# One Trainium2 core, attention into routed experts: zero rows written first, a third key buffer, a ranking matmul moved

## The chip, the cores and the metric

The kernel runs on one core of one Trainium2 chip, in one launch. The metric is the device time of an execution in microseconds; of several executions the median is taken. The profile is one execution, taken by the hardware profiler. Its times are counted from the start of the span.

## What is computed

Three layers follow one another. Batch B is 2, there are 8 heads, 768 positions and 64 elements to a head, so that a token is a row of 512.

```
# attention: only the first n_global = 8 keys and the last n_local = 96 are kept
scores = q @ k.T / 8 - slope[h] * dist          # -1e9 where a key is not kept
a      = exp(scores - max);  a /= sum(a) + 1e-9
x      = a @ v                                   # rows of 512
# mixture of 8 experts, one expert to a token
logits = x @ w_gate;  gate = sigmoid(x @ w_local)
e      = argmax(logits) where gate < 0.5 (or at the first token), else that of the token before
x      = softmax(logits)[e] * (relu(x @ w1[e]) @ w2[e])
# a channel mix of neighbouring tokens
k      = relu((mu_k x + (1-mu_k) x_prev) @ w_k)
out    = sigmoid((mu_r x + (1-mu_r) x_prev) @ w_r) * (k*k @ w_v)
```

## The kernel before, in words

The tokens are cut into 12 tiles of 128 (6 to a batch). A tile of attention has four pairs of heads; the loop at line 956 goes over the 48 pairs, `i` from 0, with `t` the tile and `h` = 0, 2, 4, 6 the first head of the pair. All instructions are put in order by hand: the block is under `manual_schedule`, so every engine runs its instructions in the order in which this code emits them, and the stages of one pair are emitted in different passes of the loop. In pass `i` come, among others:

- `emit_exp(i)`: ScalarE's exponentials. `emit_min` for pairs i+1 and i+2 (odd passes): VectorE adds the bias table to the scores and keeps the minimum. `emit_pe(i-2)`: the transposed weights are copied from PSUM, by ScalarE for every third pair, else by VectorE (L769, L771).
- `emit_qT` for a later tile (L972) and `emit_kT(t+1)` where h is 0 (L977): TensorE transposes a tile of queries or keys (L672), ScalarE copies it to `qz` (L682) or `strip` (L677). Beside them stand the loads of later tiles on SyncE's queue (L655).
- `rpop()`: one step of the routing chain (below), its part called `mid`.
- `emit_pT(i-1)`: TensorE transposes the exponentials (L757, L759) into one of two PSUM banks. On even passes then `emit_qk` for pairs i+2 and i+3, the scores (L726), into two banks that the minima must have read, and `emit_pv` for pairs i-4 and i-3, the values (L783).
- the part of the routing step called `post`, if it has one, and after it loads, GpSimd's copies of the eight global keys into `strip` (`emit_kglob`, L701, L702) and the scatter of finished rows.

The routing chain is a list of steps (L824 to L864), one taken in each pass once its tiles are done: gate matmuls (`route_lg`, L181), argmax, a scan over tokens, counts, positions. After tile 5 the experts are ranked by their count so far: `order_a` (L268) builds a key and a diagonal on VectorE, `order_b` (L277) spreads the keys with a matmul (L280) and compares, ranks and makes a one-hot on VectorE (L283 to L286); `early_start` (L801) picks the first expert by a matmul (L292), copies its number (L294), and SyncE reads it to load that expert's weights (L549) while attention still runs. `order_b` is also called a second time, by `ranks`, after all tokens.

At the head (L866 to L897), before the loop: SyncE loads the first tile's keys and queries in halves, GpSimd makes index patterns (`iotas`), VectorE and GpSimd make the bias tables (`tables0`: heads 4 to 7 on GpSimd, L515, L516), and the loads of L891 follow. `vps` are two tiles that hold, for the windows, the global keys' values and the 96 rows before a tile; their first 32 rows, and the first 24 columns of the four `peb`, are set to zero by GpSimd (L893 to L896), and `load_vp` (L658) writes into `vps` behind that. In passes 1, 5, 9 and 13 ScalarE's queue writes zeros to `xs` in DRAM, two transfers of 256 KB (L1012). Keys of a tile (128 by 512, 256 KB, in rows of 256 bytes) land in one of the `kn` buffers.

Behind the loop the first expert's tiles (`fill`), which use two of the `kn` and `qn` buffers as scratch, then all experts, then the channel mix. These have no part in the change.

Of the kernel before, what the change touches and what calls it, by code (L numbers as in the profile page):

```python
# [8 lines left out]
F32 = mybir.dt.float32  # L9
# [7 lines left out]
P = 128  # L17
B, H, S, HD = 2, 8, 768, 64
D, E, F = 512, 8, 1024
NT = S // P  # L20
NTT = B * NT
# [4 lines left out]
NG = 8  # L26
CP = WIN + NG
W = CP + P
PAD = P - CP
# [503 lines left out]
def build(ctx, tc, ins, out):  # L533
    n = Net(ctx, tc, ins, out)
    nc = tc.nc
    q, k, v = ins["q"], ins["k"], ins["v"]
# [3 lines left out]
    rp = ctx.enter_context(tc.tile_pool(name="rp", bufs=1))  # L540
# [101 lines left out]
    ap = astack.enter_context(tc.tile_pool(name="ap", bufs=1))  # L642
    X, xTs, kn, qn, vn, vhl = {}, {}, {}, {}, {}, {}

    def load(nm, t, half=None):
        b, j = divmod(t, NT)
        reg = {"k": kn, "q": qn, "v": vn}[nm]
        if half is not None:
            if half == 0:
                reg[t] = ap.tile([P, H, HD], F32, tag=f"{nm}n", bufs=2, name=f"{nm}n{t}")  # L650
            hs_ = slice(half * 4, half * 4 + 4)
            nc.sync.dma_start(out=reg[t][:, hs_, :], in_=ins[nm][b, hs_, j * P:(j + 1) * P, :].rearrange("h p d -> p h d"))
            return
        d = ap.tile([P, H, HD], F32, tag=f"{nm}n", bufs=3 if nm == "v" else 2, name=f"{nm}n{t}")
        nc.sync.dma_start(out=d, in_=ins[nm][b, :, j * P:(j + 1) * P, :].rearrange("h p d -> p h d"))  # L655
        reg[t] = d

# [168 lines left out]
    for gi, g in enumerate(groups):  # L826
        def lg(t, g=g):
            n.route_lg(g, t, xTs[t], "PT" if t == NTT - 1 else "R")
            if t == g[-1]:
                n.route_max(ap2, g)  # L830

        def fin(g=g):
            n.route_pos(ap2, g)
            scq.extend(g)
            if g[-1] == FREE - 1:
                n.cnt4 = n.early_count(rp, "cnt4")
            if g[-1] == 9:
                n.cnt9 = n.early_count(rp, "cnt9")
            if g[-1] == 7:
                n.cnte = n.early_count(rp, "cnte")  # L840

        def step(pre=None, mid=None, post=None, t=g[-1]):
            rsteps.append((t, pre, mid, post))

        max2, rows, scan, cnt = (lambda f=f, g=g: f(ap2, g) for f in (n.route_max2, n.route_rows, n.route_scan, n.route_cnt))
        if gi == 0:
            step(mid=lambda lg=lg, g=g: (lg(g[0]), lg(g[1])))
        else:
            step(mid=lambda lg=lg, g=g: lg(g[0]), t=g[0])
            step(mid=lambda lg=lg, g=g: lg(g[1]))  # L850
        if gi == 5:
            step(mid=max2, post=rows)
        else:
            step(mid=max2)
            step(mid=rows)
        step(scan)
        step(mid=cnt)
        step(post=fin)
        if g[-1] == 9:
            step(mid=early_row)  # L860
        if g[-1] == NT - 1:
            step(mid=lambda: n.order_a(rp, "f", n.clast, None))
            step(mid=lambda: n.order_b(rp, "f"))
            step(mid=early_start)  # L864

    with tc.manual_schedule():  # L866
# [5 lines left out]
        peb = [ap.tile([P, 2 * P], F32, name=f"peb{i}") for i in range(4)]  # L872
# [3 lines left out]
        vps = [ap.tile([P, D], F32, name=f"vp{i}") for i in range(2)]  # L876
# [6 lines left out]
        tstack = ExitStack()  # L883
        tp = tstack.enter_context(tc.tile_pool(name="tp", bufs=1))
        n.iotas(tp)
        n.scalars(n.const)
        tq = n.tables0(ap, tp) + n.tables(ap, tp)
        first = first_half(0)
        for _ in range(6):
            tq.pop(0)()  # L890
        for nm, a in ("k1", "q1", "v0", "v1"):  # L891
            load(nm, int(a))
        for t in vps:  # L893
            nc.gpsimd.memset(t[0:PAD + NG, :], 0.0)
        for t in peb:
            nc.gpsimd.memset(t[:, 0:PAD], 0.0)  # L896
        load_vp(1)  # L897
        NP_ = len(pairs)
        early = None
# [13 lines left out]

        def fill():
            for a in range(2):
                hn = [ap.tile([P, H, HD], F32, tag=f"{nm}n", bufs=2, name=f"hn{nm}{a}").rearrange("p h d -> p (h d)") for nm in "kq"]
                eh = [ap.tile([P, H, P], F32R, tag=tg, bufs=1, name=f"e{tg}{a}") for tg in ("tb0", "tb")]
                for u in xs_tile(0, *xe[a], hn, eh, BASES[0] + a * P):
                    if u == KF + 5:
                        early_split(1) if a == 0 else first_split()  # L920
                    for _ in range(WNEXT[u]):
                        w_next()
                    yield
# [32 lines left out]
        for i in range(NP_ + 3):  # L956
            t, h = pairs[i] if i < NP_ else (NTT + (i - NP_) // 4, 2 * ((i - NP_) % 4))
            j = t % NT
            emit_pe(i - 2, "ACT")
            if i < NP_:  # L960
                emit_exp(i, pairs[i])
            emit_xT()
            if 0 <= i - 1 < NP_:
                if pairs[i - 1][1] == H - 2:
                    n.route_ri(pairs[i - 1][0], stat[pairs[i - 1][0]][1])
            for u in (i + 1, i + 2) if i % 2 else (1,) if i == 0 else ():
                if u < NP_:
                    emit_min(u, pairs[u])
            emit_pe(i - 2, "DVE")
            rpre()  # L970
            u = {1: 1, 3: NTT, 5: 2}.get(i, t + 2 if h == 6 else NTT)
            if u < NTT:  # L972
                emit_qT(u)
                if u + 2 < NTT:
                    load("q", u + 2)
            if h == 0 and t + 1 < NTT:
                emit_kT(t + 1)  # L977
                if t + 2 < NTT:
                    load("k", t + 2)
                if t == 0:  # L980
                    load("q", 2)
            if (h == 2 or i >= NP_) and xq and xq[0] <= done_x:
                n.route_x(ap, xTs[xq[0]], X, xq[0])
                xq.pop(0)
            sct = list(scq)
            post = rpop()
            if i < 5:
                warm(NDUM[2 + i], 64)
            if 0 <= i - 1 < NP_:
                emit_pT(i - 1, pairs[i - 1])  # L990
            if i % 2 == 0:
                for u in (i + 3, i + 2):
                    if u < NP_:
                        emit_qk(pairs[u])
                for u in (i - 4, i - 3):
                    if 0 <= u < NP_:
                        emit_pv(u, pairs[u])
                        if pairs[u][1] == H - 2:
                            done_x = pairs[u][0]
            if post:  # L1000
                post()
            if i == 2:
                n.routing_consts()
            if h == 6 and t + 2 < NTT:
                load("v", t + 2)
            if h == 4 and 0 < t < NTT - 1 and (t + 1) % NT:
                load_vp(t + 1)
            if i < NP_ and j < NT - 1:
                emit_kglob(t, h // 2)
            if h == 2 and t < E // 2:  # L1010
                for e in (2 * t, 2 * t + 1):
                    nc.scalar.dma_start(out=n.xs[e * REG:e * REG + PRE, :], in_=n.warm)  # L1012
            if sct and i >= next_sc:
                next_sc = i + 1
                scatter(scq.pop(0))
            if tq:
                for _ in range(NTAB[i]):
                    if tq:
                        tq.pop(0)()
                if not tq:  # L1020
                    tstack.close()
            if i == 5:
                n.gate_rest()
            if i == 6:
                n.mix_load()
            if i == 8:
                n.mix_rest()
                n.limits(n.const)
            if i == NP_:
                early_split(0)  # L1030
            if 0 in wsrc and early is None:
                early = True
                ld_q = list(range(4))
                hi_q = [None] * 2 + [(c, s) for c in range(NIN) for s in range(2)]
            if ld_q:
                w_load(0, ld_q.pop(0))
            for u in lo_q[:1]:
                w_lo1(0, *lo_q.pop(0))
                if u[1] and u[0] < 4:
                    w_load(0, 4 + u[0])  # L1040
            if hi_q:
                u = hi_q.pop(0)
                if u:
                    w_hi1(0, *u, dve=u[1])
                    lo_q.append(u)
            if i == NP_:
                fl = fill()
            if i > NP_:
                F_(DRAINF[i - NP_])
# [192 lines left out]
    k2, sig = {}, {}  # L1242
# [129 lines left out]
    with tc.manual_schedule():  # L1372
# [48 lines left out]
        hn = ztile([P, 2, D], F32, "hn")  # L1421
# [267 lines left out]
```

## Time and profile before

| | us |
|---|---|
| median of 3 runs | 534.46 (533.41 to 535.18) |
| the profiled execution | 534.88 |
| span of the profiled execution | 533.1 |
| TensorE busy | 508.9 (95%) |
| VectorE busy | 353.3 (66%) |
| ScalarE busy | 262.1 (49%) |
| GpSimd busy | 124.9 (23%) |

PE is TensorE, PEld its weight loads, DVE VectorE, ACT ScalarE, POOL GpSimd, SP SyncE; a q behind an engine means its queue, which issues transfers. L12 is a line of the kernel. `out<-in` names the tiles that an instruction writes and reads. [...]

### The profile page before, as it was taken

Reading aid. Unit: us, or ns where it says so; the run is one execution under the profiler, and the core shown is the slowest. Engines: PE = TensorE matmul, PEld = TensorE weight load, DVE = VectorE, ACT = ScalarE, POOL = GpSimd, SP = SyncE. Lnnn points to the kernel's source line nnn. Section 1 sums busy time; section 2 is a strip of 40 time slices with the busy share of each in tenths; the row PEclk is TensorE's granted clock in tenths of the full one; section 3 lists DMA queues with packets and bytes.
Section 4 is the critical chain, followed back from the end, with each engine's and each line's share of the span. In section 5 each row is a group of like instructions: output and inputs, shape, how many; then the busy total and the mean of one; then the engine's idle time right before and its main releaser. Section 6 shows DMA issues by size and latency. Waiting matters only on the chain.

```text
span 533.1 us, 9698 instructions
## 1 busy us (share of the span) xinstructions
PE 508.9 (95%) x3375; PEld 433.4 (81%) x3375; DVE 353.3 (66%) x902; ACT 262.1 (49%) x641; POOL 124.9 (23%) x229
## 2 busy tenths in 40 slices
PE   8799998999898999999999999999999999999995
PEld 4587876777686988998989897869898989898985
DVE  6577786886743886879799899599562635444411
ACT  4567675744345454565556465575251424334130
POOL 5112122552100000000010000164172543525120
PEclk9899998979999999999999999999999999999998
DMA  7895764950158859587988976120201010110101
GB/s 136 204 184 136 153 135 112 274 186 25 61 180 276 284 178 304 165 279 229 320 257 340 309 260 256 60 61 1 80 1 59 21 59 22 42 38 1 41 1 46
DMA packets 74281, 77.03 MB, mean 144 GB/s; under 512 B 50640, under 2 KB 50896, under 8 KB 74224
## 3 DMA queue, kind: packets, MB, share of 16 engines
q1 hardware_dynamic: 65584, 52.82, 34.1%
q0 software_dynamic: 4800, 16.78, 9.4%
q10 hardware_dynamic: 3840, 6.72, 3.5%
q8 instruction: 29, 0.48, 0.4%
q14 instruction: 28, 0.23, 0.2%
HBM read 63.30 MB, written 13.01 MB: 143 GB/s over the span
## 4 chain that ended last, share of the span: by engine, by line
PE 71%; DVE 15%; DMA 8%; issue 2%; ACT 1%; POOL 0%; SPq 0%; DVEq 0%; ACTq 0%; POOLq 0%
PE O L589 8%; PE O L591 8%; PE O L590 8%; PE S L589 6%; PE S L591 6%; PE S L590 6%; PE S L726 4%; DVE wlo L586 4%; PE O L783 4%; DMA dw<-in_moe_w_v_dram 3%; PE PT L591 3%; PE PT L590 3%; PE PT L589 3%; PE PT L757 2%; PE R L181 2%
## 5 line engine op out<-in xcount | busy, mean ns | idle before, releaser
L577 ACT ACTIVATE whi<-wraw 128x512 fp32r<-128x512 f32 x116 | 67.1, 624 | 23.7 <-DMA wraw<-in_moe_w_dram 19.4
L586 DVE TENSOR_TENSOR wlo<-wraw,whi 128x1024 fp32r<-128x1024 f32 x54 | 65.8, 1219 | 5.0 <-ACT whi L577 4.8
L1252 ACT ACTIVATE rl<-S 128x256 f32<-128x256 f32 x48 | 18.5, 385 | 80.4 <-PE S L591 80.2
L589 PE MATMUL S<-xkh,whi 128*128 128x256 f32 x192 | 54.5, 284 | 0.4 <-DVE sq L1254 0.4
L590 PE MATMUL S<-xkl,whi 128*128 128x256 f32 x192 | 53.6, 279 | 0.6 <-DVE xkl L1230 0.6
L591 PE MATMUL S<-xkh,wlo 128*128 128x256 f32 x192 | 53.7, 280 | 0.0
L1262 POOL TENSOR_TENSOR kl<-sq,kh 128x256 fp32r<-128x256 f32 x40 | 32.0, 808 | 80.1 <-ACT kh L1261 80.1
L748 ACT ACTIVATE peb<-sc,nm 128x232 f32<-128x232 f32 (+1 forms) x96 | 44.3, 464 | 12.2 <-PE PT L759 7.7
L1292 DVE TENSOR_TENSOR o<-O,sig 128x512 f32<-128x512 f32 (+1 forms) x13 | 8.5, 651 | 61.3 <-PE O L591 34.5
L738 DVE CUSTOM_DVE_ANT_0 sc<-S,tb 128x232 f32<-128x232 f32 (+1 forms) x94 | 30.2, 376 | 14.5 <-PE S L726 13.1
L589 PE MATMUL O<-whi,kh 128*128 128x512 f32 (+1 forms) x104 | 39.2, 377 | 0.0
L590 PE MATMUL O<-wlo,kh 128*128 128x512 f32 (+1 forms) x104 | 39.2, 377 | 0.0
L591 PE MATMUL O<-whi,kl 128*128 128x512 f32 (+1 forms) x104 | 39.2, 377 | 0.0
L589 PE MATMUL O<-whi,hh 128*128 128x512 f32 x96 | 38.0, 396 | 0.0
L590 PE MATMUL O<-wlo,hh 128*128 128x512 f32 x96 | 37.9, 395 | 0.0
L591 PE MATMUL O<-whi,hl 128*128 128x512 f32 x96 | 37.9, 395 | 0.0
L590 PEld LDWEIGHTS S<-xkl,whi 128*128 128x128 f32 x192 | 36.1, 188 | 1.0 <-DVE xkl L1230 0.8
L1254 DVE SCALAR_TENSOR_TENSOR sq<-S,rl 128x256 f32<-128x256 f32 x48 | 19.9, 420 | 25.7 <-ACT rl L1252 25.0
L589 PEld LDWEIGHTS S<-xkh,whi 128*128 128x128 f32 x192 | 36.0, 187 | 0.9 <-DVE sq L1254 0.6
L591 PEld LDWEIGHTS S<-xkh,wlo 128*128 128x128 f32 x192 | 36.0, 188 | 0.0
L589 PE MATMUL S<-xh,whi 128*128 128x256 f32 (+1 forms) x96 | 28.0, 292 | 0.0
L589 PE MATMUL PT<-xh,whi 128*128 128x256 f32 (+1 forms) x96 | 27.9, 291 | 0.0
(348 smaller groups left out, 1411.2 us busy)
## 6 DMA issues: line engine op xcount, KB each, us to landing
wraw<-in_moe_w_dram SPq DMA_DIRECT2D x64, 512.0 KB, 4.7
ys<-yo ACTq DMA_DIRECT2D x17, 256.0 KB, 5.3
dw<-in_moe_w_k_dram POOLq DMA_DIRECT2D x8, 512.0 KB, 4.7
dw<-in_moe_w_v_dram POOLq DMA_DIRECT2D x8, 512.0 KB, 5.5
xn<-xs SPq DMA_DIRECT2D x14, 256.0 KB, 5.2
vn<-in_v_dram SPq DMA_DIRECT2D x12, 256.0 KB, 4.5
kn<-in_k_dram SPq DMA_DIRECT2D x11, 256.0 KB, 4.9
qn<-in_q_dram SPq DMA_DIRECT2D x11, 256.0 KB, 4.0
```

The lines of the kernel that those rows point to most:

```text
L577: nc.scalar.activation(out=whl[r, c][0][:, sl], in_=raws[r, c][:, sl], func=ACTF.Copy)
L586: nc.vector.tensor_tensor(lo, raws.pop((r, c)), hi.bitcast(F32), op=ALU.subtract)
L589: nc.tensor.matmul(out_, lhsT=ah, rhs=bh, start=first, stop=False)
L590: nc.tensor.matmul(out_, lhsT=ah, rhs=bl, start=False, stop=False)
L591: nc.tensor.matmul(out_, lhsT=al, rhs=bh, start=False, stop=last)
L726: nc.tensor.matmul(ps[a], lhsT=qz[t % 2][a * HD:(a + 1) * HD, p, :], rhs=strip[a * HD:(a + 1) * HD, p, k0:k0 + N], start=True, stop=True)
L738: nc.vector.tensor_tensor_reduce(out=sc[:, c0:W], in0=ps[a], in1=(n.tb if t % NT else n.tb0)[:, h + a, :], scale=1.0, scalar=3.0e38, op0=A ...
L748: nc.scalar.activation(out=pe[:, PAD + c0:2 * P], in_=sc[:, c0:W], func=ACTF.Exp, scale=-1.0, bias=nm[:, h + a:h + a + 1], accum_out=sm[:, ...
L783: nc.tensor.matmul(Os[t][a * HD:(a + 1) * HD, p * P:(p + 1) * P], lhsT=v_src(t, c)[:, (h + a) * HD:(h + a + 1) * HD], rhs=pt[:, (2 * c + a ...
L1252: nc.scalar.activation(out=rl, in_=ps[:, 0:TB], func=ACTF.Relu)
L1254: nc.vector.scalar_tensor_tensor(sq_, ps[:, 0:TB], 0.0, rl, op0=ALU.max, op1=ALU.mult)
L1262: (nc.gpsimd if b else nc.vector).tensor_tensor(hl, sq_, hh.bitcast(F32), op=ALU.subtract)
```

## The change

GpSimd's memsets move from behind the first table operations and loads to right behind the index patterns. The key tiles get three buffers instead of two. The third tile's keys (`k2`) are loaded right behind `v0`, ahead of `v1` and `load_vp(1)`; in the loop, each pass with h = 0 then loads the keys of tile t+3 instead of t+2, in the first pass behind the load of `q2`. The routing step of `order_b` becomes a `post` step: its matmul stands behind the transposes, scores and values of its pass instead of ahead of them. The two scratch tiles of `fill` name the same number of buffers.

```diff
@@ load (both places; fill alike)
-                reg[t] = ap.tile([P, H, HD], F32, tag=f"{nm}n", bufs=2, name=f"{nm}n{t}")
+                reg[t] = ap.tile([P, H, HD], F32, tag=f"{nm}n", bufs=2 if nm == "q" else 3, name=f"{nm}n{t}")
...
-        d = ap.tile([P, H, HD], F32, tag=f"{nm}n", bufs=3 if nm == "v" else 2, name=f"{nm}n{t}")
+        d = ap.tile([P, H, HD], F32, tag=f"{nm}n", bufs=2 if nm == "q" else 3, name=f"{nm}n{t}")
@@ routing steps
             step(mid=lambda: n.order_a(rp, "f", n.clast, None))
-            step(mid=lambda: n.order_b(rp, "f"))
+            step(post=lambda: n.order_b(rp, "f"))
             step(mid=early_start)
@@ head
         n.iotas(tp)
+        for t in vps:
+            nc.gpsimd.memset(t[0:PAD + NG, :], 0.0)
+        for t in peb:
+            nc.gpsimd.memset(t[:, 0:PAD], 0.0)
         n.scalars(n.const)
         tq = n.tables0(ap, tp) + n.tables(ap, tp)
         first = first_half(0)
         for _ in range(6):
             tq.pop(0)()
-        for nm, a in ("k1", "q1", "v0", "v1"):
+        for nm, a in ("k1", "q1", "v0", "k2", "v1"):
             load(nm, int(a))
-        for t in vps:
-            nc.gpsimd.memset(t[0:PAD + NG, :], 0.0)
-        for t in peb:
-            nc.gpsimd.memset(t[:, 0:PAD], 0.0)
         load_vp(1)
@@ loop
             if h == 0 and t + 1 < NTT:
                 emit_kT(t + 1)
-                if t + 2 < NTT:
-                    load("k", t + 2)
                 if t == 0:
                     load("q", 2)
+                if t + 3 < NTT:
+                    load("k", t + 3)
```

## Rows read from the trace of the kernel before

**Rows 1.** The page's busy times of the engines.

```profile
PE 508.9 (95%) x3375; PEld 433.4 (81%) x3375; DVE 353.3 (66%) x902; ACT 262.1 (49%) x641; POOL 124.9 (23%) x229
```

**Rows 2.** TensorE's waits, whole span: us in total, times, longest.

```profile
PE O L672 <- DMA kn<-in_k_dram: 3.8, 1, 3.8
PE R L280 <- DVE dgf L275: 2.4, 1, 2.4
```

**Rows 3.** SyncE's queue in order of time: start us, us.

```profile
11.11 0.35 SPq L662 DMA_DIRECT2D vp<-in_v_dram  x1
...
93.59 0.43 SPq L655 DMA_DIRECT2D kn<-in_k_dram  x1
```

**Rows 4.** GpSimd in order of time at the head; in brackets idle time before.

```profile
6.41 0.33 POOL L515 TENSOR_SCALAR tb<-d 128x128 f32<-128x128 f32 x1 [4.27 <-DVE d L506]
...
10.10 0.98 POOL L894 MEMSET vp<- 32x512 f32 x2
11.03 0.27 POOL L896 MEMSET peb<- 128x24 f32 x4
...
20.89 0.48 POOL L124 COPY wgb<-wg 64x36 f32<-64x36 f32 x2 [7.06 <-DMA wg<-in_moe_w_local_dram]
```

**Rows 5.** Stretches: length, busy by engine, then granted clock, transfer share, GB/s.

```profile
4.00:11.00 7.00, 6.33 (x41) 3.67 (x40) 5.43 (x26) 3.04 (x11) 4.17 (x10) 1.00 1.14 212
11.00:12.00 1.00, 1.00 (x12) 0.94 (x9) 1.00 (x10) 0.99 (x5) 0.88 (x9) 1.00 0.01 1
12.00:18.00 6.00, 2.10 (x17) 1.40 (x16) 4.02 (x25) 2.97 (x13) 1.68 (x8) 1.00 1.10 246
...
18.40:21.60 3.20, 3.20 (x20) 2.18 (x19) 0.65 (x5) 1.92 (x6) 0.59 (x4) 0.50 0.82 160
...
86.60:90.00 3.40, 3.40 (x23) 2.44 (x23) 1.67 (x10) 1.53 (x5) 1.27 (x4) 0.50 0.20 77
...
111.00:117.00 6.00, 6.00 (x35) 5.00 (x35) 4.70 (x19) 2.59 (x9) 4.56 (x4) 0.50 0.45 175
```

**Rows 6.** The chain that ended last, 0 to 30 us: start us, us, what.

```profile
11.93 5.75 DMA kn<-in_k_dram
...
17.72 0.66 PE O L672 x4
...
18.64 0.43 PE PT L757 x2
...
21.92 0.59 PE T L672 x4
```

**Rows 7.** VectorE in order of time at the head.

```profile
15.24 0.42 DVE L771 COPY pt<-PT 128x256 f32<-128x256 f32 x1
```

**Rows 8.** The same chain, 76 to 110 us.

```profile
81.10 1.02 PE O L783 x16
...
84.42 0.60 DVE pt L771
...
86.08 0.19 PE R L280 x2
...
86.98 1.85 PE S L726 x8
88.83 1.60 PE O L783 x16
...
93.44 1.03 PE S L726 x8
```

**Rows 9.** VectorE in order of time around the ranking.

```profile
86.87 0.44 DVE L286 TENSOR_SCALAR Rf<-iota_e,rkf 8x8 f32<-8x8 f32 x1
88.97 0.40 DVE L738 CUSTOM_DVE_ANT_0 sc<-S,tb 128x232 f32<-128x232 f32 x1 [1.66 <-PE S L726]
...
91.18 0.14 DVE L294 CAST fi<-R 1x1 int32<-1x1 f32 x1 [0.84 <-PE R L292]
```

**Rows 10.** ScalarE's first weight split, in order of time.

```profile
97.59 0.63 ACT L577 ACTIVATE whi<-wraw 128x512 fp32r<-128x512 f32 x1 [3.22 <-DMA wraw<-in_moe_w_dram]
```

More of the change, by code (lines that the diff above doesn't have):

```diff
@@ L915, in fill @@
             for a in range(2):
-                hn = [ap.tile([P, H, HD], F32, tag=f"{nm}n", bufs=2, name=f"hn{nm}{a}").rearrange("p h d -> p (h d)") for nm in "kq"]
+                hn = [ap.tile([P, H, HD], F32, tag=f"{nm}n", bufs=2 if nm == "q" else 3, name=f"hn{nm}{a}").rearrange("p h d -> p (h d)") for nm in "kq"]
                 eh = [ap.tile([P, H, P], F32R, tag=tg, bufs=1, name=f"e{tg}{a}") for tg in ("tb0", "tb")]
```

## The prediction

> **What bounds the kernel now.** The page first: TensorE is busy for 508.9 us of a span of 533.1 [rows 1], so time can only come from the places where it waits or runs slowly. The waits of TensorE, longest first, give two that stand alone at the top [rows 2]: 3.8 us in the key transpose of L672 for the transfer of a key tile, and 2.4 us in the ranking matmul of L280 for VectorE. Both belong to lines that the change touches.
>
> The chain of waits at the head shows the first one [rows 6]: the third tile's keys are issued at 11.93, land 5.75 us later, and TensorE goes on at 17.72, so it stopped at 13.94. SyncE's queue says why the issue is so late [rows 3]: the load of `vp` in front of it left only at 11.11, when GpSimd had written the zero rows (10.10 to 11.08) behind its four tables [rows 4]. In that time the transfer engines had nothing to do: share 1.14 from 4 to 11 us, 0.01 from 11 to 12 [rows 5].
>
> [...]
>
> **The sum, part by part.** It is made against the profiled execution, 534.88 us with a span of 533.1 us; the median of the runs shown is 534.46, that is 0.42 less. About 0.3%, 1.6 us, is what a measurement of this kernel can tell from no change.
>
> *Zero rows before the tables.* Two memsets of 0.98 us together and four of 0.27 us together move into the 4.27 us in which GpSimd waits for its first table operand [rows 4]. Cost nothing; if that cover were gone, 1.25 us on the tables, which VectorE's first minima would see. The tables cannot start sooner, since VectorE's `d` ends their wait. GpSimd's copies behind them come up to 1.25 us sooner, which gives nothing: VectorE is busy without a gap until its copy that ends at 15.66 [rows 7].
>
> *Third key buffer, third key tile ahead of v1 and vp.* No load is added: `k2` moves from behind `vp` to the place of `v1` in SyncE's queue, `v1` and `vp` one place back, and from then on each key tile is asked for one tile earlier. Six loads of 262 kB, halves counted together, end by about 11 us in the trace of before (212 GB/s over 7 us is 1,484 kB [rows 5]). In the new order the sixth is `k2`, so it is there about 3 us before TensorE asks at 13.94. The first stop is gone as such. What is late next: the key transposes take 0.66 us [rows 6] to 14.6; then the transposes of pair 3 need the PSUM bank that VectorE frees at 15.66 [rows 7]; they take at most 0.43 [rows 6], to 16.1; scores 1.03, to 17.1; eight value matmuls, half of the 1.02 that sixteen take [rows 8], to 17.6. With some 0.1 us between the blocks the transpose of `q2` can start at 18.0, where before it started at 21.92 [rows 6]: **3.9 us**. In this the clock is in: 3.2 us at 0.50 are no longer there, as TensorE now rests for about a microsecond instead of 3.8.
>
> The next transfer asked for is `q2`. From 11 us the queue still has to move v1, vp and q2 (262+213+262 kB), and the two zero-fill transfers of ScalarE's queue (524 kB) come between: 1,261 kB at 246 GB/s [rows 5] is 5.1 us, so 16.1 at best. By the same count `k2` in the trace of before should have landed at 16.1 from 12 us on (999 kB) and landed at 17.68, 1.6 late [rows 6]; with the same lateness `q2` comes at 17.7. So it is just in time for 18.0; a further microsecond late leaves 2.9. I take 3.9, with bounds of 2.9 and 4.3. [...] The gate weights, behind one more key load, land about 1.1 us later in absolute time; GpSimd's copies, which waited to 20.89 for them [rows 4], are then done near 22.5. The first scores that read them stand behind another block of scores, two of transposes and one of values after 18.0, so past 23. Nothing there.
>
> *The other key loads.* Each leaves one tile sooner into a buffer already free. The last one leaves SyncE's queue from between two expert-weight loads (0.43 us of issue at 93.59 [rows 3]). ScalarE's 3.22 us wait for the first such weights [rows 10] shortens a little; it is not on the chain. Nothing. Fill's two scratch tiles only rotate through three buffers.
>
> *Ranking matmul behind the scores.* Before, it stood in front of the transposes of pair 33 and held them until it had run at 86.08 [rows 8]. Behind them, they need only the PSUM bank freed by VectorE's copy (84.42 + 0.60 = 85.02 [rows 8]). New order from there: transposes to 85.6, scores to 86.7, values (1.02) to 87.75, then the ranking matmul. That is 1.1 us sooner for the scores, and TensorE rests 1.4 us instead of 2.4; I take the full clock to hold; no row settles it, so the bounds hold both. But the change adds a wait on VectorE: comparison, rank and one-hot, which ended at 87.31 [rows 9], now wait for a matmul that comes at 87.75 instead of 86.08 [rows 8], and the minima of pairs 36 and 37 stand behind them. From matmul to the end of the one-hot was 1.23 us, so 88.98: the minima start at 89.0 where they started at 88.97 [rows 9]. VectorE gains nothing. TensorE's pick matmul waits for the one-hot (89.05), the index copy stands behind the four minima of about a third of a microsecond each (90.4 instead of 91.18), and the gate matmuls need its bank: 90.6 to 91.4, transposes to 91.9, next scores at 92.0 where they were at 93.44 [rows 8]: **1.4 us**. Bounds: had the clock fallen anyway, the same steps with 1.85 for the scores and 1.60 for the values end near 93.4, so 0 (down to -0.5 with the index later); were VectorE not held, 2.6. [...]
>
> Sum: 3.9 + 1.4 = 5.3, so 529.6 for an execution like the profiled one, **529.2 us** for the median. Beyond 117 us the clock is full and TensorE busy, so the shift should carry to the end.
>
> **The rivals.**
>
> *A, a third slow stretch goes too.* From 111 to 117 us the granted clock is 0.50 as well [rows 5], in a part with many narrow gate matmuls and short rests, which the change does not touch but shifts. 6 us at half clock cost about 3 us of matmul time, of which VectorE would give back some: 2.5 less, 526.7. For it: nothing there waits long, so it may hang on alignment. Against: the same instructions follow in the same order.
>
> *B, the ranking gives nothing.* The clock falls in the 1.4 us rest all the same, or the held minima eat the gain: 530.6. For: the sum above already shows VectorE with nothing gained.
>
> *C, the wait moves to `q2`* (the load order does only part of what it says). `v1`, `vp` and the zero fills stand before it. Gain of the head 1.9 to 2.9: 530.2 to 531.5. Against: all loads up to `q2` together start into engines that idled for a microsecond before.
>
> [...]
>
> **How the numbers follow.** Forecast 0.52, A 0.17, B 0.15, C 0.11, D 0.05. The forecast's own range is 528.0 to 530.6. The range asked for leaves out D, the far half of A and the far end of C: 526.2 to 532.0. Faster by over 0.3% (below 532.9) holds for forecast, A, B and nearly all of C: 0.92. Within 0.3%: 0.04 (both gains at their low ends). Slower by over 0.3%: 0.04.
>
> **What would show it.** Right: no wait of TensorE for a key transfer at the head; the issue of `vp` before 10 us; the transfer share without a hole at 11 us; granted clock 1.00 from 18 to 22; the transpose of `q2` near 18.0; no wait before L280; a new VectorE wait of about 1.5 us in front of L283; the scores after the ranking about 5.3 us sooner than 93.44. [...]

## The result, and the profile after

The changed kernel takes **529.42 us** (median of 4 runs, 528.31 to 529.60) against 534.10 us for the kernel before on the same chip; the ratio is 0.991, with a 95% interval of 0.988 to 0.993. 529.2 us had been forecast. The profiled execution took 529.60 us (before: 534.88), its span is 527.8 us (before: 533.1), so 5.3 us are gone from the trace as well. By the medians the gain is 4.7 us.

The page's busy times of the kernel after [rows 1]:

```profile
PE 506.8 (96%) x3375; PEld 431.5 (82%) x3375; DVE 354.9 (67%) x902; ACT 262.4 (50%) x641; POOL 124.3 (24%) x229
```

Waits of TensorE in the kernel after, whole span (us in total, times, longest). Both waits of [rows 2] are gone. One in front of the ranking is 1.5 us long, and a small one for GpSimd's strip copy is new:

```profile
PE PT L757 <- DVE pt L771: 1.5, 1, 1.5
...
PE S L726 <- POOL strip L702: 0.3, 1, 0.3
```

**The head.** SyncE's queue of the kernel after (start us, us): the third tile's keys leave at 6.80, `vp` at 9.26 instead of 11.11 [rows 3], `q2` right behind at 10.57.

```profile
6.80 1.01 SPq L655 DMA_DIRECT2D kn<-in_k_dram  x1
...
9.26 0.83 SPq L662 DMA_DIRECT2D vp<-in_v_dram  x1
```

GpSimd in order of time (in brackets the idle time before). Both groups of memsets run in the wait for the first table operand, which shrinks from 4.27 to 3.24 us; the table operation starts at 6.51 instead of 6.41 [rows 4].

```profile
2.07 0.97 POOL L887 MEMSET vp<- 32x512 f32 x2
3.00 0.27 POOL L889 MEMSET peb<- 128x24 f32 x4
6.51 0.32 POOL L515 TENSOR_SCALAR tb<-d 128x128 f32<-128x128 f32 x1 [3.24 <-DVE d L506]
...
20.55 0.48 POOL L124 COPY wgb<-wg 64x36 f32<-64x36 f32 x2 [6.67 <-DMA wg<-in_moe_w_local_dram]
```

TensorE in order of time. The key transpose (L672, `kn`) no longer waits; the next stop is 1.28 us in front of the transposes of L757; the transpose of `q2` starts at 17.84, where it started at 21.85 in this view (21.92 in the chain of [rows 6], which dates it a little later in either kernel).

```profile
13.87 0.60 PE L672 MATMUL O<-ident,kn 128*128 128x128 f32 x4
...
15.92 0.41 PE L757 MATMUL PT<-ident,peb 128*128 128x128 f32 x2 [1.28 <-DVE RI L172]
16.26 1.05 PE L726 MATMUL S<-strip,qz 64*128 64x232 f32 x8
...
17.84 0.66 PE L672 MATMUL T<-ident,qn 128*128 128x128 f32 x4
```

**The stretches** of [rows 5] in the kernel after (columns as there; third from the end stands the granted clock, TensorE's, with 1.00 for its full speed, and behind it the time that packets took as a share of 16 transfer engines' time). The hole in the transfers at 11 us is filled, the clock is full from 18 to 22 and behind the ranking. But it is 0.50 from 64.4 to 67.8, where before it was not, and in the third stretch only for 3.4 us.

```profile
11.00:12.00 1.00, 1.00 (x10) 1.00 (x11) 1.00 (x10) 1.00 (x5) 0.88 (x6) 1.00 1.30 212
...
18.40:21.60 3.20, 3.20 (x32) 2.56 (x31) 2.12 (x10) 2.72 (x10) 0.86 (x5) 1.00 1.01 243
64.40:67.80 3.40, 3.40 (x23) 2.72 (x24) 1.33 (x9) 1.12 (x6) 1.61 (x5) 0.50 0.24 92
86.60:90.00 3.40, 3.25 (x28) 2.81 (x30) 2.15 (x12) 2.66 (x9) 0.00 (x0) 1.00 0.45 109
108.80:112.20 3.40, 3.40 (x25) 2.42 (x23) 3.37 (x11) 1.00 (x5) 2.74 (x3) 0.50 0.67 231
```

**The ranking.** TensorE of the kernel after, in order of time. The scores of pass 34 (L726, 83.67) stand in front of the ranking matmul (L280, 85.69), which waits for nothing, and take 1.05 us at the full clock, where they took 1.92 before in this view (1.85 in the chain of [rows 8]).

```profile
83.12 0.30 PE L757 MATMUL PT<-ident,peb 128*128 128x128 f32 x1 [1.49 <-DVE pt L771]
...
83.67 1.05 PE L726 MATMUL S<-strip,qz 64*128 64x232 f32 x8
...
85.69 0.20 PE L280 MATMUL R<-dgf,ones 8*8 8x8 f32 x2
...
89.44 1.05 PE L726 MATMUL S<-strip,qz 64*128 64x232 f32 x8
```

VectorE beside it: the comparison waits 1.45 us for that matmul, and the one-hot (L286) and the minima of the next pairs (L738) stand behind it [rows 9].

```profile
85.92 0.21 DVE L283 TENSOR_SCALAR gtf<-R,keyf 8x8 f32<-8x8 f32 x1 [1.45 <-PE R L280]
...
86.35 0.22 DVE L286 TENSOR_SCALAR Rf<-iota_e,rkf 8x8 f32<-8x8 f32 x1
86.49 0.38 DVE L738 CUSTOM_DVE_ANT_0 sc<-S,tb 128x232 f32<-128x232 f32 x1
```

**Where the 5.3 us come from.** The same blocks of scores (L726), start in us:

| scores | before | after | sooner by |
|---|---|---|---|
| behind the transpose of `q2` | 23.31 | 19.29 | 4.0 |
| three blocks on | 36.58 | 32.93 | 3.65 |
| before the stretch at 64 us | 68.06 | 64.41 | 3.65 |
| behind it | 72.75 | 70.69 | 2.1 |
| last block with the transposes of the ranking still ahead | 80.04 | 77.99 | 2.05 |
| behind the ranking | 93.37 | 89.44 | 3.9 |
| before the third stretch | 106.33 | 102.51 | 3.8 |
| the last of all | 113.95 | 108.56 | 5.4 |

So: head 4.0, lost 0.35 by 33 us, lost 1.6 at 64 to 68, ranking 1.9, third stretch 1.6. The shift does not simply hold from there. The next matmuls that need VectorE (L221) come 4.8 us sooner, since TensorE waits longer for them. The kernel before:

```profile
119.46 0.38 PE L221 MATMUL R<-ident,ab 128*1 128x128 f32 x2 [0.61 <-DVE ab L211]
```

And the kernel after:

```profile
114.64 0.38 PE L221 MATMUL R<-ident,ab 128*1 128x128 f32 x2 [1.17 <-DVE ab L211]
```

TensorE stays 4.7 to 4.9 us ahead until 310 us, and the span ends 5.3 sooner mainly because a later wait, 1.26 us for VectorE at 332.85 in the kernel before, is absent after. What was lost at 64 us shows instruction by instruction. The kernel before, TensorE in order of time:

```profile
68.06 1.05 PE L726 MATMUL S<-strip,qz 64*128 64x232 f32 x8
69.04 0.44 PE L783 MATMUL O<-pt,vn 128*64 128x128 f32 x4
...
70.07 0.66 PE L672 MATMUL T<-ident,qn 128*128 128x128 f32 x4
```

The kernel after, the same instructions: scores 1.92 instead of 1.05 us, four value matmuls 0.69 instead of 0.44.

```profile
64.41 1.92 PE L726 MATMUL S<-strip,qz 64*128 64x232 f32 x8
66.26 0.69 PE L783 MATMUL O<-pt,vn 128*64 128x128 f32 x4
...
68.01 0.65 PE L672 MATMUL T<-ident,qn 128*128 128x128 f32 x4
```

### The profile page after: what moved, and what is told of

Its sections match the earlier page's. It is cut to its first block, busy times and chain, and to the rows that moved or that the text cites. A ratio compares the mean times of both kernels' runs of the same rounds, so it can differ in the third digit from the quotient of the medians.

```text
span 527.8 us, 9693 instructions
## 1 busy us (share of the span) xinstructions
PE 506.8 (96%) x3375; PEld 431.5 (82%) x3375; DVE 354.9 (67%) x902; ACT 262.4 (50%) x641; POOL 124.3 (24%) x229
## 4 chain that ended last, share of the span: by engine, by line
PE 76%; DVE 10%; DMA 6%; issue 2%; ACT 2%; SPq 1%; POOL 1%; ACTq 0%; DVEq 0%; POOLq 0%
PE O L589 9%; PE O L591 9%; PE O L590 9%; PE S L591 7%; PE S L589 7%; PE S L590 7%; PE PT L591 4%; PE PT L590 4%; PE PT L589 4%; PE O L783 3%; PE S L726 3%; DMA dw<-in_moe_w_v_dram 3%; PE PT L757 2%; PE R L181 2%; DVE sc L738 2%
## 5 line engine op out<-in xcount | busy, mean ns | idle before, releaser
L738 DVE CUSTOM_DVE_ANT_0 sc<-S,tb 128x232 f32<-128x232 f32 (+1 forms) x94 | 30.2, 375 | 9.7 <-PE S L726 9.7
```

The source lines that it names most:

```text
L738: nc.vector.tensor_tensor_reduce(out=sc[:, c0:W], in0=ps[a], in1=(n.tb if t % NT else n.tb0)[:, h + a, :], scale=1.0, scalar=3.0e38, op0=A ...
```

## The experiments

Twelve kernels (two of them the changed one again), four at a time on one chip, each set beside runs of the kernel before (medians there: 535.84, 535.28 and 534.16 us). A "ratio" is to that kernel on the same chip. The traces of one group also differ by waits that no edit here touches, so a part is read from the distance of its own instructions and not from the span. The theory: the head gives some 4 us and the ranking some 1.5, and the clock's other stretches merely move. The rivals: the third key buffer carries the head; the ranking gives nothing; the stretches belong to the kernel and are part of its gain or loss.

### Single parts of the change

**The ranking step put back** in the changed kernel.

```
-            step(post=lambda: n.order_b(rp, "f"))
+            step(mid=lambda: n.order_b(rp, "f"))
```

> The changed kernel with the ranking matmul back in front of the transposes. Theory (head 4.0 us, ranking 1.9 us in the trace after): 1.4 to 1.9 us slower than the changed kernel, 530.9 to 531.3; TensorE waits 2.4 us before L280 again. Rival (the ranking gives nothing, the rest of the gain is where the slow-clock stretches fall): 529.4.

Measured: 531.27 us (528.93 to 536.24, 4 runs), ratio 0.988 [0.983, 0.992]. The time lies in the expected window, but the kernel before is 1.7 us slower on this chip, and by the ratio this kernel is not slower than the whole change (0.991); the times show no loss. In its trace both things at the ranking are back. The 2.4 us among TensorE's waits of this kernel:

```profile
PE R L280 <- DVE dgf L275: 2.4, 1, 2.4
```

And the half clock in the stretch behind it:

```profile
85.20:88.40 3.20, 3.20 (x24) 2.29 (x20) 1.37 (x8) 1.49 (x5) 0.33 (x3) 0.50 0.24 90
```

**The ranking step moved alone**, everything else as before (the line above, the other way round).

> The kernel before with the ranking step alone moved. Theory: 1.4 to 1.9 us faster than before, 532.2 to 532.7; scores of pass 36 about 1.9 us sooner than 93.4, the 3.8 us stop at the head unchanged. Rival (ranking gives nothing): 534.1.

Measured: 532.70 us (529.22 to 537.47, 7 runs), ratio 0.991 [0.987, 0.996]. From the scores of pass 32 to those of pass 36 it takes 11.6 us, against 13.3 before and 13.3 with the step put back. The stretch behind the ranking runs at the full clock:

```profile
85.00:88.40 3.40, 3.04 (x36) 2.30 (x32) 1.72 (x10) 2.33 (x8) 1.42 (x4) 1.00 0.44 126
```

So the move is worth 1.7 to 1.9 us in place, in either surrounding. (At the head, the key wait was 2.0 us long in this trace, not 3.8 as expected.) The rival that it gives nothing falls in place; by the times alone it would not.

**The zero rows first, alone**: key buffers, order of loads and ranking as before.

```
         n.iotas(tp)
+        for t in vps:
+            nc.gpsimd.memset(t[0:PAD + NG, :], 0.0)
+        for t in peb:
+            nc.gpsimd.memset(t[:, 0:PAD], 0.0)
```

(the four lines are taken out behind the loads)

> The kernel before with the zero rows alone written first; two key buffers, the third keys behind vp. Theory (either of the two head edits is enough, since the queue only has to be free): vp leaves by 9, the third keys by 10 and land near 13, before TensorE asks at 13.9; 3.5 to 4 us faster than before, 530.1 to 530.6. Rival (the third buffer and the place ahead of vp are needed): the stop shrinks to 1 to 2 us and the gain is 2 us or less, 532 or more.

Measured: 531.75 us (529.83 to 535.46, 10 runs), ratio 0.992 [0.989, 0.996]. The median lies between the two windows, 4.1 us below the kernel before on this chip. SyncE's queue of this kernel: `vp` leaves at 8.04 and the third tile's keys at 9.39, still behind it.

```profile
8.04 0.60 SPq L662 DMA_DIRECT2D vp<-in_v_dram  x1
...
9.39 0.80 SPq L655 DMA_DIRECT2D kn<-in_k_dram  x1
```

TensorE of this kernel: the transpose waits 0.40 us for them.

```profile
14.20 0.66 PE L672 MATMUL O<-ident,kn 128*128 128x128 f32 x4 [0.40 <-DMA kn<-in_k_dram]
...
16.15 1.05 PE L726 MATMUL S<-strip,qz 64*128 64x232 f32 x8
```

The scores at 16.15 are those that the whole change has at 16.26. The rival that the third buffer is needed for the head falls: the four moved lines of memsets are enough.

**The key loads alone**: third buffer and new order, zero rows late, ranking as before (the diff of the change without its memsets and without its ranking line).

> The kernel before with the key loads and the third buffer alone; the zero rows stay behind the tables, the ranking where it was. Theory: the third keys land near 11.8, but the queries of the third tile stand behind vp, which still leaves at 11.1, so they land at 17.5 to 18.5 and TensorE, which asks at 17.8, waits 0 to 0.7 us; 3.2 to 4 us faster than before, 530.1 to 530.9. Rival (the wait moves to the queries as a whole): a stop of 2 us or more for qn, gain of 2 us or less, 532 or more.

Measured: 534.59 us (531.32 to 542.33, 10 runs), ratio 0.997 [0.994, 1.001]: no gain that can be told from none, where 3.2 to 4 us had been expected. The key wait at the head is gone here too, and the scores stand at 16.14 and 19.17, as with the whole change; so either of the two edits ends that stop. A new wait stands in its place at 29 us. SyncE's queue of this kernel in order of time:

```profile
23.36 0.83 SPq L119 DMA_DIRECT2D muk<-in_moe_mu_k_dram  x1
```

GpSimd of this kernel:

```profile
28.44 0.20 POOL L128 TENSOR_SCALAR muk<-muk 128x4 f32<-128x4 f32 x1 [6.56 <-DMA muk<-in_moe_mu_k_dram]
...
28.82 0.44 POOL L702 COPY strip<-glob 128x8 f32<-128x8 f32 x3
```

And TensorE:

```profile
29.07 1.92 PE L726 MATMUL S<-strip,qz 64*128 64x232 f32 x8 [2.20 <-POOL strip L702]
```

GpSimd waits for the small `mu` loads in L128, its copies of the global keys into `strip` stand behind that wait, and TensorE's scores wait 2.20 us for the copies. The scores then run at 1.92 us for eight: the clock was 0.50 from 28.9. The `mu` loads leave hardly sooner than in the kernel before (23.36 against 23.87), while TensorE comes to these scores 4 us sooner; before, they started at 30.93, right behind copies that ended at 30.65. With the zero rows alone the `mu` loads leave at 20.99 and L128 runs at 25.08, with the whole change at 21.94 and 26.07 (26.0 to 27.3 in the seven traces with both parts). So the one key load more in front is worth 1 to 2 us of the lateness, the late `vp` the rest. Neither the queue nor the wait appears in what the change says it touches.

### The whole change again, and without its key part

**The changed kernel unchanged, on the second chip.**

> The changed kernel once more, on the chip of the three kernels beside it, as the base for their times. Expected: 529.4 us (528.3 to 530.5); in the trace the granted clock 0.50 for 3.4 us from about 64 and for 3.4 us from about 109 us. If those two stretches are chance of one execution and not of the kernel, they will stand elsewhere here, or last 6.8 us.

Measured: 530.38 us (528.16 to 531.07, 6 runs), ratio 0.990 [0.987, 0.993]. Stretches of this trace:

```profile
64.40:67.80 3.40, 2.93 (x31) 2.16 (x30) 2.00 (x11) 2.31 (x10) 1.72 (x6) 1.00 0.22 86
108.80:112.20 3.40, 2.52 (x30) 1.84 (x26) 3.40 (x11) 1.04 (x5) 2.77 (x3) 1.00 0.64 228
115.30:118.60 3.30, 3.30 (x23) 2.56 (x19) 1.50 (x5) 1.85 (x6) 0.00 (x0) 0.50 0.15 52
```

Both stretches of the first trace are at the full clock; one of 3.4 us stands at 115 instead. The clock's pattern is not a property of the instructions alone. What this execution saved it lost elsewhere. Its scores of pass 8 waited 1.29 us for `strip`, the wait that the key part brings. From 64 to 70 us it gained 1.6 on the first trace. The full clock at 109 gained nothing, for TensorE then waited for VectorE in L221, 2.85 us instead of 1.17, and 0.50 followed that rest:

```profile
114.17 0.38 PE L221 MATMUL R<-ident,ab 128*1 128x128 f32 x2 [2.85 <-DVE ab L211]
```

**The changed kernel on the third chip.**

> The changed kernel a third time, as the base for the three kernels beside it. Expected: 529.9 us (528.5 to 531). Two traces of this kernel so far show the granted clock 0.50 at 64.4 and 108.8 us in the one, at 115.2 us alone in the other. If the places hang on how the execution lies and not on the instructions, a third trace shows a third pattern, with no 0.50 behind the ranking matmul and at most 6.9 us in all before 120 us.

Measured: 530.06 us (529.82 to 532.21, 6 runs), ratio 0.994 [0.991, 0.996]. The pattern is the first one again (0.50 from 64.7 and from 109.0 us, 3.4 us each), so the third pattern expected did not come; no 0.50 stands behind the ranking.

**Without the key part**: the kernel before with the zero rows first and the ranking behind.

> The zero rows first and the ranking matmul behind, on the kernel before, without the third key buffer and the new order of key loads. Theory (the two other edits carry the whole gain): the same time as the changed kernel within 0.15%, 528.6 to 530.2; at the head the third tile's keys are waited for by less than 0.5 us, the scores of pair 4 start near 16.1 and those of the next pairs near 19.2 us, as with the zero rows alone; no TensorE wait for a strip copy of GpSimd, since the mu loads leave SyncE sooner; no 0.50 at the ranking. Rival (the key part carries a part of the gain): 530.5 us or more, with a key wait of TensorE over 1 us at the head.

Measured: 530.92 us (527.58 to 534.53, 12 runs), ratio 0.992 [0.989, 0.996], beside 530.38 for the changed kernel on the same chip. The forecast window of 528.6 to 530.2 was missed by its median, and the times spread wide; by times the two can't be told apart. By the trace TensorE waits neither for the third tile's keys nor for `strip` (it came 1.8 us late to both, so this says less than the 0.40 us with the zero rows alone). TensorE at its head: this execution's first scores came late (14.14 for the block that the changed kernel has at 12.3), but from there the blocks follow at 3.97 and 3.03 us, as in the changed kernel (3.92 and 3.03).

```profile
9.02 1.89 PE L879 MATMUL O<-warm 128*128 128x512 f32 x2
...
14.14 1.05 PE L726 MATMUL S<-strip,qz 64*128 64x232 f32 x8
...
18.11 1.05 PE L726 MATMUL S<-strip,qz 64*128 64x232 f32 x8
```

The lateness is in matmuls that took nearly twice their time (the two of L879 above take 1.02 us in the changed kernel). By 134 us (L241) this kernel is 0.6 us behind the first trace of the changed kernel and 0.2 behind the second. What makes its span of 530.2 longer comes later, in a load of routed rows in the first expert's tiles, with 0.50 for 3.4 us behind it:

```profile
164.72 1.11 PE L1116 MATMUL T<-ident,xn 128*128 128x128 f32 x4 [2.61 <-DMA xn<-xs]
```

In the three traces of the changed kernel that wait is 0.3 to 0.7 us. It was 3.44 us long with the ranking put back, a kernel that has the key part, so it is no sign of the missing key part; its cause is open. So the key part adds nothing that these traces show; that it costs something in the median isn't shown either.

### Where VectorE holds the path

**The VectorE half of the ranking one pass later**, behind the minima.

```
-            step(post=lambda: n.order_b(rp, "f"))
+            step(post=n.order_m)
+            step(mid=lambda: n.order_b(rp, "f", n.kp))
```

(`order_m` is the matmul of `order_b`)

> The changed kernel with the VectorE half of the ranking (comparison, rank, one-hot) taken out of the pass of its matmul and put into the next pass, behind the minima; the picking of the first expert and what follows in the routing chain come a pass later. Theory (the hold of VectorE in front of the comparison, 1.45 us in the changed kernel, is on the path, as the forecast's price of the ranking said): the minima of pairs 36 and 37 start near 85.0 instead of 86.5 us and the scores behind the ranking come 1.0 to 1.4 us sooner than 89.4: 528.6 us, 1.2 below the base beside it. Rival (the minima are not what sets those scores): the minima start sooner and the scores stay at 89.4 within 0.3; the time stays within 0.4 us of the base.

Measured: 531.20 us (529.33 to 533.86, 12 runs), ratio 0.995 [0.993, 0.997]: 1.1 us above the changed kernel beside it by the medians, with overlapping intervals. In place the theory holds, in the time it does not. VectorE of this kernel, the first minimum and the comparison:

```profile
83.02 0.40 DVE L743 CUSTOM_DVE_ANT_0 sc<-S,tb 128x232 f32<-128x232 f32 x1 [0.40 <-ACT peb L753]
...
84.31 0.21 DVE L288 TENSOR_SCALAR gtf<-R,keyf 8x8 f32<-8x8 f32 x1
```

The minima no longer wait for the matmul, and from scores to scores it takes 10.0 us (76.15 to 86.12) instead of 11.45. But every later routing step comes a pass later, and at the end of attention nothing is left to hide it. TensorE's waits show it, 2.0 and 1.7 us where the changed kernel has 0.5 and 0.6:

```profile
PE R L260 <- DVE mm L249: 2.0, 2, 1.2
PE R L181 <- DVE cnte L303: 1.7, 1, 1.7
```

The clock, 0.50 for 6.8 us from 106.0, took another part back. A hold moved out of one place was paid for at the end of a chain that has no slack, 2.6 us in these two waits against 1.5 gained.

**The VectorE half of the position step one pass later** (same split for `route_pos` of tiles 4 and 5; no step is added to the chain, since the half rides in front of `order_a`).

```
-        step(post=fin)
+        if gi == 2:
+            step(post=lambda g=g: n.route_pm(ap2, g))
+        else:
+            step(post=fin)
...
+            def pos(g=g):
+                n.route_pr(ap2, g)
+                scq.extend(g)
+            step(pre=pos, mid=lambda: n.order_a(rp, "f", n.clast, None))
```

> The changed kernel, with the VectorE half of the position step for tiles 4 and 5 moved from behind its matmul in one pass to the start of the next pass, behind the minima. It tests whether the 1.49 us that TensorE waits in pass 34, ahead of the ranking, comes from VectorE being held by that matmul. Theory: VectorE is held 1.44 us there, the minima and the copy of the weights then come about as much sooner, the wait of L757 at 83 us falls under 0.5 us and the scores at 83.7 come near 82.6: 1.0 us, 528.4 us. Rival (VectorE has no slack there, its work only changes places): the scores of pass 34 come sooner, but the wait stands in the next pass, before the ranking matmul, and the time is 529.4 us within 0.4.

Measured: 529.38 us (527.74 to 530.52, 6 runs), ratio 0.989 [0.986, 0.992]; the changed kernel beside it has 530.38. The time is the one that the rival gave (529.4), the trace is the theory's. TensorE of this kernel: the scores of pass 34 come 4.00 us behind those of pass 32, without a wait, where the changed kernel takes 5.68 (77.99 to 83.67).

```profile
76.41 1.05 PE L733 MATMUL S<-strip,qz 64*128 64x232 f32 x8
...
80.41 1.05 PE L733 MATMUL S<-strip,qz 64*128 64x232 f32 x8
...
86.17 1.05 PE L733 MATMUL S<-strip,qz 64*128 64x232 f32 x8
```

The wait did not move into the next pass (5.76 us there, 5.77 before). The third stretch of this execution was 6.8 us long again (0.50 from 103.8). Even so it is 2.4 us ahead of the first trace of the changed kernel at 131 us (L241 at 131.24 against 133.65); most of that goes at the load of routed rows, where 0.50 follows again for 3.4 us, and 0.6 us are left in its span of 527.2.

```profile
161.46 0.78 PE L1130 MATMUL T<-ident,xn 128*128 128x128 f32 x4 [2.48 <-DMA xn<-xs]
```

### The clock, and the strip copies

**Two added matmuls** of 256 columns, read by nobody, in the rests ahead of the stretches at 64 and 109 us.

```
+        def fillT(m=256):
+            nc.tensor.matmul(n.bank("T", 1)[:, 0:m], lhsT=n.warm[:, 0:P], rhs=n.warm[:, 0:m], start=True, stop=True)
...
+            if i in DUMT:
+                fillT()
...
+            if i in DUMP:
+                fillT()
```

(`DUMT` is pass 26, `DUMP` pass 42)

> The changed kernel with two added matmuls (256 columns, read by nobody) at the two places where TensorE waits shortly before the slow stretches at 64 and 109 us. Theory (the clock falls after what TensorE rests there, so a matmul in the rest keeps it up): no 0.50 in 62 to 68 us and none in 108 to 113; each stretch is worth about 1.6 us (the shift lost at 64 to 68, and what the shorter third stretch gained), the added matmuls cost 0.3 us each where they do not fit the wait: 526.8 us (526 to 528). Rival (the stretches are not set by these rests): both stay where they are or move a few us, and the time is 529.4 to 530.4 us.

Measured: 532.05 us (529.88 to 536.50, 12 runs), ratio 0.995 [0.992, 0.998]: 1.7 us slower than the changed kernel beside it, and not the 526.8 expected. No 0.50 stands at 64 or at 109 in its trace, one of 3.4 us at 115.6; but the changed kernel showed just that on the same chip without them, so what keeps the clock up stays open. The first of the two had itself to wait 0.70 us at 65.5 for VectorE to free the PSUM bank it writes into.

**The operations on `mu` six passes later.**

```
+            if i == 14:
+                n.mix_rest()
             if i == 8:
-                n.mix_rest()
                 n.limits(n.const)
```

> The changed kernel with GpSimd's two operations on mu (L128) six passes later, so that its copies of the global keys no longer stand behind them. Theory (the wait of TensorE for the strip copy, 0.3 and 1.3 us in two traces of the changed kernel and 2.2 with the key part alone, is GpSimd standing behind the mu load): no TensorE wait for strip in any trace; the scores of pair 8 stay 4.1 us behind those of pair 6 (27.3 after 23.2, where the disturbed trace has 28.2 after 23.0); median 0.8 us below the base, 529.1 us. Rival (the copies were late for another reason, or TensorE meets its next wait): the same wait is there, or the gain is gone by 33 us, and the time stays within 0.3 us of the base.

Measured: 529.21 us (526.80 to 531.04, 6 runs), ratio 0.990 [0.987, 0.993], 0.85 below the changed kernel beside it; the spreads overlap. There is no wait for `strip`, and the scores of pass 8 start 3.76 us behind those of pass 6, and not 4.1 as expected: that figure (23.16 to 27.28 in the first trace of the changed kernel) held 0.30 us of the wait. With 1.29 us of it, in the second trace, it is 5.1. That the `mu` load is what GpSimd stands behind is shown: its copies, three of which ran at 27.04 behind L128, are all done by 24.5 here. (One trace that keeps the old place, that of the ranking's half moved, has no wait for `strip` either; there L128 ran at 26.02.)

**Both**, the position step and `mu`.

> The changed kernel with the position step's VectorE half a pass later (as in the run for that alone) and the operations on mu six passes later. Theory (the two are independent, and the first is worth 2.5 us in place by its trace, of which a slow stretch took some back): no wait of L757's transposes at 83 us, no wait for strip, the scores behind the ranking at 86 us where the changed kernel has 89: 527.4 us, 2.5 below the base beside it. Rival (the part in front of the ranking only trades its waits against the clock): the scores come sooner, the third slow stretch lasts 6.8 us again, and the time is 529.0 to 529.6 us, less than 1 us below the base.

Measured: **527.08 us** (525.96 to 530.89, 6 runs), ratio 0.989 [0.985, 0.993], with the changed kernel at 530.06 (529.82 to 532.21) beside it. Its span is 525.2 us, and the scores behind the ranking start at 87.2 (expected 86), with 0.50 at 64.6 and at 105.6 for 3.4 us each. It has the lowest median of all; four of its six runs lie below every run of the changed kernel, two between. It beats the kernel before; over the changed kernel its lead of some 3 us rests on medians and on the two waits that its trace no longer has; 2.2 to 2.5 us can be placed (L241 at 131.41, against 133.65 and 133.94 in the two traces of the changed kernel with 0.50 at much the same places).

## Why the prediction was right

The total came out, and so did three landmarks (head 4.0, ranking 1.9, no fall of the clock behind the ranking); every run of the changed kernel but one (532.21 against 532.0) lies in the range. A fourth did not: the scores behind the ranking came 3.9 us sooner and not about 5.3. That the sum hits within 0.3 us is luck, since losses and gains that it did not hold cancel. By the medians the gain is 4.7 us here and 4.9 and 4.1 on the other two chips. Point by point:

- **Memsets at no cost: right.** 1.24 us of memsets went into a wait that gave 1.03 of its length; L515 starts 0.1 us later.
- **Head 3.9 us: right, 4.0 at the scores and at the transpose of `q2`** (forecast for 18.0, came at 17.84). The place of the next stop was right too: the PSUM bank that VectorE frees by a copy (L771) that ends at 15.78, 1.28 us; the profile names the instruction next to the copy, L172. `q2` was not late, so rival C falls. SyncE's earlier issue filled engines that had been idle for a microsecond, share 0.01 then and 1.30 now. Behind the stop of 1.28 us the granted clock was 1.00 from 18.4 to 21.6; it had been 0.50 behind the one of 3.78 [rows 5], and was 0.50 from 17.0 to 20.4 behind the 2.0 us of the ranking step moved alone. That the shorter stop is the cause was the author's estimate.
- **Credit for the head: not separated.** The prediction took the third buffer and the earlier key load as what ends the stop. Zero rows first does it alone, for `vp` and `k2` behind it then leave 3.1 and 2.5 us sooner; the key loads do it alone too, and lose it again at 29 us.
- **"The other key loads: nothing": wrong, by 0.3 us in the first and third trace and 1.3 in the second.** The step had looked at the buffers and at the queue's late end, and not at what stands right behind the extra load at 18 us: the `mu` loads, for which GpSimd waits with the strip copies behind it.
- **Gate weights later, GpSimd's copies near 22.5: wrong and harmless.** They came at 20.55, before 20.89.
- **Ranking 1.4 us: mechanism right, term too small by 0.5.** From the forecast's own start, 2.05 us earlier by then, the matmul should stand at 85.70; it stood at 85.69. The rest of 1.4 us measured 1.49, the clock stayed full, and the comparison waited 1.45 us. The mis-sized term is "from matmul to the end of the one-hot 1.23 us": now the one-hot (86.35, 0.22 long) ends 0.88 us behind the matmul. In the row before it took 0.44 us, and VectorE came to the comparison late from a copy. Why it took twice as long is open (0.42 to 0.44 in all four traces with the old order, 0.22 to 0.24 in the ten with the new). So the minima start at 86.49 where the working gives 86.95, and the scores at 89.44 where it gives 89.95. That the minima stay behind the waiting comparison, as the working took it, the trace shows: their scores were there by 84.7, and they began at 86.49 behind it; in the run with the VectorE half a pass later, where the comparison stands behind them, they began at 83.02.
- **The clock behind the ranking, taken to hold: right, and shown.** 0.50 stands between 84 and 91 us in all four traces with the old order of that step and in none of the ten with the new. Rival B falls, and so does D, the chance of 0.05 of a slower kernel. The low bound's 1.85 and 1.60 us are blocks of [rows 8] that ran at 0.50 [rows 5].
- **"The shift carries to the end": right only as a sum.** The prediction saw no stretch at 64 us (loss 1.6) and gave rival A, the third stretch, 2.5 us for going whole; it was halved, a gain of 1.6, of which the longer wait in L221 took back 0.6. The shift of 4.8 us became 5.3 by a wait of 1.26 us at 332.85 that is absent after. Where the stretches lie is not fixed by the change: the second trace of the same kernel has neither, and 3.4 us at 115. Their sum may be in part: the third stretch was 6.8 us in all four traces with the old ranking and in three of the ten with the new. The mean granted clock of a whole execution says the same: 0.985 over 62 of the kernel before (0.974 to 0.993), 0.993 over 16 of the changed one (0.990 to 0.996). That is some 9 us less at 0.50 in 530 (an estimate from these means), where the two stretches of before behind the stops [rows 5] are 6.8, 3.4 each. With the zero rows alone the mean is 0.985 in ten executions, so the clock that the head gave back was lost elsewhere (0.50 from 64.0 in its trace); with the ranking alone it is 0.990 in seven. Why the clock falls in one execution and not in another stays open; the one attempt to hold it up was inconclusive.
- **"Beyond 117 us the clock is full and TensorE busy": so in most traces, not in all.** Three of the fourteen (ranking put back, key part left out, position step later) have a wait of 2.5 to 3.4 us for routed rows that ends between 161 and 168 us, and 0.50 for 3.4 us behind it.
- **Two slips in the working, without effect on the forecast.** "1.1 us sooner for the scores" is 1.4 by the times beside it (85.6 against 86.98; the trace gives 1.2), and rival C's upper end should be 531.2 for a head gain of 1.9, not 531.5.

The times of single parts do not add up: the zero rows alone (ratio 0.992) and the ranking alone (0.991) together would exceed the whole (0.990 to 0.994). With intervals of 0.3 to 0.4% each, and a clock that takes 1.6 us here and there, only their places in the traces, 4.0 and 1.9 us, can be told.

## What to carry to other kernels

A stop at the head was ended by moving six memsets into a wait that was there anyway: look first for what an issuing queue waits on, before adding buffers. Whoever puts a load ahead must read on along the queue to the next small load behind it, and along the engine that waits for that one; here the wait for such a load cost TensorE 0.3 to 1.5 us in six of the seven traces with the whole key part, the zero rows first and `mu` in its old place, and 2.2 with the zero rows late. And a wait taken from an engine's path is worth what stands behind it only if the moved work is not at the end of a chain: the same split gained 1.7 us in place for one routing step and 1.5 for the next, but the second was lost again in later waits (1.1 us slower in the end, by medians whose intervals overlap).

## What the runs showed of the hardware

- The granted clock differs between executions of one kernel. The changed kernel had 0.50 from 64.4 and 108.8 us in one trace, from 64.7 and 109.0 in another, and from 115.2 alone in the third. A block of eight scores took 1.05 us or 1.92 by it, so that up to 1.6 us in place can come or go without any edit.
- The fall of the clock behind the ranking belonged to the order: after a rest of 2.4 us it fell in each of four traces, after one of 1.5 in none of the eight that had it. It also fell behind the rests of 2.8 to 2.9 us in L221 (three traces, 0.50 from 115 us). A long rest is not the whole of it: from 64.4 us in the changed kernel it was 0.50 with no rest of over 0.5 us in the 9 us before.
- In the trace without the key part, matmuls from 7.4 to 10.9 us took 1.6 to 1.9 times their usual time (0.80 against 0.49 for four scores, 1.89 against 1.02 for the two of L879) while the granted clock is given as 1.00. Slow matmuls there can't be read from that column; their durations show them.
